# Batch 0 of a fused attention and maxout kernel: part of its up layer as block products, one PSUM copy in another place, its scores in 64x64 tiles

## The chip, the cores and the metric

The kernel runs on one core of a Trainium2 chip, as one launch. The metric is the device time of one execution in microseconds. The kernel before takes 320.29 us, the median of three runs (320.01 to 320.5).

## The reference

For each of 8 batches, 8 heads, 1024 positions and 64 features per head, keys and values are projected from 1024 positions to 64, attention runs over the 64 projected ones, and the heads are joined to rows x of 512 features. A layer of two products, their maximum and a third product follow.

```python
k_proj = np.einsum('ks,bhsd->bhkd', E, k)
v_proj = np.einsum('ks,bhsd->bhkd', F, v)
scores = scale * np.matmul(q, k_proj.transpose(0, 1, 3, 2))
...
attn = np.exp(scores)
attn = attn / (np.sum(attn, axis=-1, keepdims=True) + 1e-09)
x = np.matmul(attn, v_proj)
...
h1 = x @ w1
h2 = x @ w2
g = np.maximum(h1, h2)
out = g @ w_out
```

x has 8192 rows of 512 features, w1 and w2 are 512x1024, w_out is 1024x512, all inputs and the output float32. The kernel computes in float16 with float32 sums.

## The kernel before

**The algebra.** max(h1, h2) is written as relu(h1 − h2) + h2. So the kernel makes wd = w1 − w2 (`step_wd`, `step_wd_rows`), the *up layer* relu(x·wd), and M = w2·w_out once (`m_steps`); the *down layer* is relu(x·wd)·w_out + x·M, with x and the relu'd block joined along the contraction. For M, w2 is turned by TensorE transposes into a PSUM bank, and copied from there into `w2t_sb` by ScalarE (`step_w2t`, 256 of the 1024 columns at a time).

**Seven block products.** M, the down layer, and the up layer of batches 1 to 7 are computed by a scheme of the Strassen kind: both factors are cut into 2x2 blocks, seven products of sums of blocks replace the eight plain ones. They are called p1 to p7 and issued in the order 1, 2, 6, 5, 7, 3, 4. Three PSUM accumulators X, Y and Z hold them: X takes products 1, 6, 7 and 4 on top of each other and is copied to SBUF after each of the first three (`keep`, by ScalarE, into float32 tiles `p_sb`), Y takes product 2, Z products 5 and 3. VectorE adds the copies and the banks to the four result blocks. VectorE also prepares the sums: those of the weights once (`step_t` for w_out and M, `step_tw` for wd), those of x and of the relu'd block for every half batch (`sums_x`, `sums_g`), those of the turned w2 once (`sums_m`). In `up_steps` such a layer is done in two parts, d = 0 and d = 1: part d makes the columns of blocks 2d, 2d+1 (of 128) of either half of the 1024.

**Batch 0** is different: its up layer runs in the plain form (`up_slots`), eight blocks `u0[0]` to `u0[7]` for its first half of positions and `u1[0]` to `u1[7]` for the second, each of 4 matmuls of 128x128 against 512 columns into one bank, followed by a relu on ScalarE (on VectorE for block 3). The down layers of its two halves are `down_steps` of the units U[0, 0] and U[0, 1].

**PSUM.** Four banks are taken by `mm_bank`, by turns or by number, two double banks by turns by `att_banks`. A bank is written again only when its reader has finished.

**Order.** The order in which each engine issues is the program's order: the kernel is scheduled by hand. The list `slots` holds the steps of the steady part one after another; `at_slot` hangs further steps (sums, batch 1's attention, loads) behind a slot. The first 26 us (attention of batch 0) are written out line by line, with matmuls on ones (`warm`) between them. The list begins after that, with the rest of batch 0's up layer, the transposes of w2, and M; then the down layer of U[0, 0] follows in slots named ("P", 0, ...), with batch 1's attention hung behind them.

**Scores.** `score` computes exp's argument for four heads and 256 positions: for each head, both halves of the position tiles (`o`), a weight tile of the projected keys of 64 rows is cut into two of 32 columns, and each of these 16 tiles is a matmul of 64x32 against 256 columns. The 16 outputs lie in two banks. `step_sc` runs it for batches 0 and 1, `step_group` for the later ones.

**Transfers.** POOL's queue issues the loads: k, q, v of batch 0, the weights w2 and w1 in pieces, w_out, then batch 1's k, v, q and batch 2's k. SP's queue issues the check of the sums, the transposes of q by DMA in later batches, and the stores.

**Scratch.** `big0` to `big3` are SBUF tiles of 16 KB per partition. `big1` and `big2` first hold w1 and w2; after M's inputs are made, `open_box` takes them again under the same names for the sums (`s_g`, `s_x`), `big0` for the sums of wd (`t_w`), and `big3` holds `w2t_sb` and later sums of x.

## Time and profile before

| | |
|---|---|
| median of the runs | 320.29 us (320.01 to 320.5) |
| the profiled execution | 320.29 us, of which its span takes 318.5 us |
| TensorE (PE) busy | 311.8 us of the span |
| VectorE (DVE) busy | 241.1 us |
| ScalarE (ACT) busy | 206.0 us |
| granted TensorE clock | full speed in all 40 slices of the span |
| moved by DMA | 53.71 MB, 169 GB/s on average |

The profile is that of one execution. Its span runs from the first to the last record on the core; the time of the execution is 1.8 us more. A row of the chain of waits names the work that the end depended on, in order of time; a row of a timeline names an engine's instructions in order, with the idle time before them and what ended it in square brackets. "x16" is a count; "busy" includes the tail of a pipelined matmul, so that the rows of the chain, which do not overlap, are the ones to add up.

### The profile page before, as it was taken

The numbers are of one execution on the slowest core, as the hardware profiler recorded it, in microseconds if no ns is written. First come the engines' busy times: TensorE is split into PE (matmuls) and PEld (weight loads), VectorE is DVE, ScalarE is ACT, GpSimd is POOL, SyncE is SP. The second block draws the span as 40 slices with busy tenths as digits, with TensorE's granted clock in tenths as the row PEclk, the third lists the DMA queues.
The fourth block names the chain that finished last, engine by engine and source line by source line (L and its number), as shares of the span: only waits on it lengthen the run. The fifth ranks groups of instructions, "written<-read, shape, count | busy, mean of one in ns | idle before, by whom it ended". The sixth has DMA issues, their size and how long they took to land.

```text
span 318.5 us, 9309 instructions
## 1 busy us (share of the span) xinstructions
PE 311.8 (98%) x3922; PEld 253.8 (80%) x3922; DVE 241.1 (76%) x442; ACT 206.0 (65%) x373; POOL 41.4 (13%) x63
## 2 busy tenths in 40 slices
PE   7999999999999999999999999999999999999996
PEld 3565588888887888788887888788887888888885
DVE  2366889887969696896969696996969696969883
ACT  2386742777776777477776777477776777765541
POOL 8259102004000300012000400030000000000000
PEclk9999999999999999999999999999999999999999
DMA  7999999999989999799999999989979131313124
GB/s 179 206 202 197 207 207 201 207 156 141 204 163 183 171 209 245 208 188 147 225 229 219 169 199 245 221 155 174 230 153 217 42 101 36 102 35 102 36 99 136
DMA packets 76684, 53.71 MB, mean 169 GB/s; under 512 B 29664, under 2 KB 76128, under 8 KB 76640
## 3 DMA queue, kind: packets, MB, share of 16 engines
q0 software_dynamic: 30688, 28.05, 56.0%
q1 hardware_dynamic: 45664, 24.85, 33.1%
q8 instruction: 31, 0.51, 0.6%
q10 hardware_dynamic: 288, 0.20, 0.2%
q14 instruction: 13, 0.11, 0.1%
HBM read 57.15 MB, written 16.78 MB: 232 GB/s over the span
## 4 chain that ended last, share of the span: by engine, by line
PE 95%; DMA 3%; ACT 1%; DVE 1%; issue 0%; POOLq 0%
PE mm_ps L838 47%; PE mm_ps L746 27%; PE mm_ps L525 4%; PE mm_ps L195 4%; PE att_ps L352 4%; PE mm_ps L340 2%; DMA k_sb<-in_k_dram 2%; PE mm_ps L634 2%; PE att_ps L237 1%; PE mm_ps L311 1%; PE mm_ps L153 1%; DMA out_dram<-o_sb 1%; PE att_ps L340 0%; DVE qt_sb L316 0%; ACT ld_sb L388 0%
## 5 line engine op out<-in xcount | busy, mean ns | idle before, releaser
L720 ACT COPY p_sb<-mm_ps 128x512 f32<-128x512 f32 x179 | 101.7, 592 | 49.2 <-PE mm_ps L746 27.3
L838 PEld LDWEIGHTS <-big 128*128 128x128 f16 x768 | 73.5, 98 | 11.8 <-issue 3.6
L838 PE MATMUL mm_ps<-T_sb,big 128*128 128x256 f16 x576 | 76.9, 273 | 0.0
L761 DVE TENSOR_TENSOR gt_sb<-mm_ps,p_sb 128x512 f16<-128x512 f32 x56 | 38.5, 688 | 43.0 <-PE mm_ps L746 41.6
L746 PE MATMUL mm_ps<-big,big 128*128 128x256 f16 x336 | 50.4, 273 | 0.0
L746 PEld LDWEIGHTS <-big 128*128 128x128 f16 x448 | 43.8, 98 | 5.1
L838 PE MATMUL mm_ps<-wo_sb,gt_sb 128*128 128x256 f16 x256 | 42.6, 273 | 0.0
L838 PEld LDWEIGHTS <-gt_sb 128*128 128x128 f16 x376 | 35.7, 98 | 6.7 <-issue 2.7
L469 ACT ACTIVATE ex_sb<-mm_ps 128x512 f16<-128x512 f32 x50 | 27.2, 597 | 18.0 <-PE mm_ps L340 12.3
L746 PEld LDWEIGHTS <-wd_sb 128*128 128x128 f16 x336 | 32.9, 98 | 3.8
L746 PE MATMUL mm_ps<-xt_sb,wd_sb 128*128 128x256 f16 x224 | 32.8, 273 | 0.0
L499 DVE TENSOR_TENSOR xt_sb<-att_ps,ld_sb 128x1024 f16<-128x1024 f32 x26 | 31.7, 1219 | 0.2
L303 POOL COPY junk<-qt_sb 1x1 f16<-1x1 f16 x6 | 2.6, 432 | 172.3 <-DMA qt_sb<-q_sb 172.3
L838 PE MATMUL mm_ps<-m_sb,xt_sb 128*128 128x256 f16 x128 | 24.4, 273 | 0.0
L869 DVE TENSOR_TENSOR o_sb<-mm_ps,p_sb 128x512 f32<-128x512 f32 x32 | 21.9, 683 | 2.8 <-ACT p_sb L898 2.0
L764 DVE TENSOR_SCALAR gt_sb<-gt_sb 128x512 f16<-128x512 f16 (+1 forms) x60 | 20.9, 348 | 2.1
L706 DVE TENSOR_TENSOR big<-gt_sb 128x1024 f16<-128x1024 f16 x32 | 21.9, 683 | 0.0
L838 PE MATMUL mm_ps<-wo_sb,big 128*128 128x256 f16 x128 | 21.5, 273 | 0.0
L807 ACT ACTIVATE gt_sb<-mm_ps 128x512 f16<-128x512 f32 x28 | 16.8, 601 | 5.7 <-PE mm_ps L746 5.7
L838 PE MATMUL mm_ps<-T_sb,gt_sb 128*128 128x256 f16 x120 | 20.3, 273 | 0.0
L838 PEld LDWEIGHTS <-xt_sb 128*128 128x128 f16 x188 | 18.3, 98 | 2.3 <-issue 0.2
L761 DVE TENSOR_TENSOR gt_sb<-p_sb 128x512 f16<-128x512 f32 x28 | 19.1, 682 | 0.6 <-ACT p_sb L720 0.6
(121 smaller groups left out, 434.8 us busy)
## 6 DMA issues: line engine op xcount, KB each, us to landing
out_dram<-o_sb SPq DMA_DIRECT2D x62, 256.0 KB
k_sb<-in_k_dram POOLq DMA_DIRECT2D x7, 1024.0 KB, 9.7
v_sb<-in_v_dram POOLq DMA_DIRECT2D x7, 1024.0 KB, 15.4
q_sb<-in_q_dram POOLq DMA_DIRECT2D x5, 1024.0 KB, 22.8
q_sb<-in_q_dram POOLq DMA_DIRECT2D x6, 512.0 KB, 15.9
big<-in_moe_w_dram POOLq DMA_DIRECT2D x12, 128.0 KB, 6.4
v_sb<-in_v_dram POOLq DMA_DIRECT2D x4, 256.0 KB, 14.0
wo_sb<-in_moe_w_out_dram POOLq DMA_DIRECT2D x1, 1024.0 KB, 10.4
```

Source lines behind the costliest of these rows:

```text
L195: nc.tensor.matmul(out=kv_ps[r * KP : (r + 1) * KP, h * D : (h + nh) * D], lhsT=eft[i][:, c, :], rhs=t[w][:, h0 + h : h0 + h + nh, c, :], ...
L352: nc.tensor.matmul(out=dst(r ^ (hh % 2))[hh * Z : (hh + 1) * Z, :], lhsT=weights(rows, hh), rhs=ex[rows, hh % 2, hh // 2 * W : (hh // 2 + ...
L469: nc.scalar.activation(out=t["ex", g, j][:, e, :], in_=banks[e], func=ACTF.Exp, scale=scale)
L499: nc.vector.tensor_tensor(out=x_out(t, g, j).rearrange("q z o n -> q o z n"), in0=at_ps.rearrange("q o (z n) -> q o z n", z=2), in1=ld[:, ...
L706: nc.vector.tensor_tensor(out=S(i), in0=S(0) if x is None else x, in1=y(), op=op)
L720: copy(out=x, in_=bank)
L746: nc.tensor.matmul(out=bank[:, m * W : (m + 1) * W], lhsT=w_[:, n_, (2 * d + m) * 128 : (2 * d + m + 1) * 128], rhs=a[:, n_, :], start=(n ...
L761: nc.vector.tensor_tensor(out=c_blk(j, c), in0=two(x), in1=two(y), op=ALU.add)
L764: nc.vector.tensor_scalar_max(ap, ap, 0.0)
L807: nc.scalar.activation(out=out, in_=in_, func=ACTF.Relu)
L838: nc.tensor.matmul(out=bank[i][:, 0:CH] if two_banks else bank[:, i * CH : (i + 1) * CH], lhsT=a(c)[:, i * 128 : (i + 1) * 128], rhs=w_(c) ...
L869: nc.vector.tensor_tensor(out=o_sb, in0=two(x), in1=two(y), op=ALU.add)
```

## The change

Four things change, all in the part for batch 0 and M.

1. **Scores.** For batch 0 alone, `score` uses tiles of 64 columns, so that a call has 8 matmuls of 64x64 against 256 columns instead of 16 of 64x32. The other batches keep 32.
2. **Up layer.** Blocks 2, 3, 6 and 7 of `u1` are gone. They are computed by the seven products S1 to S7 of part d = 1 of `up_steps` for the unit U[0, 1]. Their copies go to tiles of the pool `soft` instead of `ppool`. S2's add and relu are held back (`c0`) and run as a slot of their own; the adds that follow S3 are held back too (`rest`) and run behind a slot of the down layer. The other blocks of batch 0 now take the banks 0 and 1 by turns (`fb % 2`), the products the banks 2 and 3.
3. **Order.** w2's second half (columns 512 to 1023) is turned earlier, right after S2, into the double banks; the second of its two copies by ScalarE is held back (`hold`) and issued behind the relu of `u0[4]`. Sums of x for U[0, 1], the differences of wd for d = 1 (`step_tw` now takes one part at a time), the sums for M and the differences of w_out stand in the list itself; sums for U[0, 0] move behind M's first products, and the differences of wd for d = 0 to the slots where U[0, 1]'s sums of x were. M's product 1 takes a double bank instead of bank 2, its product 2 bank 0, and its first add comes after product 6 (`M_add`).
4. **Scratch.** `s_g` and `s_x` lie in fixed columns of w1 and w2 instead of reopened tiles, since w1 and w2 are still partly read when the first sums are written.

```diff
@@ -335,11 +335,12 @@ score
-                    for s in range(2):
-                        pos = D * (o ^ e) + s * Z
+                    z = D if t is tiles[0] else Z
+                    for s in range(0, D, z):
+                        pos = D * (o ^ e) + s
                         nc.tensor.matmul(
-                            out=banks[e][pos : pos + Z, h * W : (h + 1) * W],
-                            lhsT=kpt_of(t, head, o)[:, s * Z : (s + 1) * Z],
+                            out=banks[e][pos : pos + z, h * W : (h + 1) * W],
+                            lhsT=kpt_of(t, head, o)[:, s : s + z],
...
@@ -518,7 +519,7 @@ up_slots
-                    t["up", j, fb] = mm_bank(n=None if r1 == NDC else first_banks[j][fb])
+                    t["up", j, fb] = mm_bank(n=first_banks[j][fb] if r1 < NDC else fb % 2)
...
@@ -560,9 +561,16 @@ step_w2t(f0, att=False, hold=False)
-        nc.scalar.copy(
-            out=w2t_sb[:, fb : fb + 2, :].rearrange("q f m -> q (f m)"), in_=ps_t
-        )
+
+        def copy():
+            nc.scalar.copy(
+                out=w2t_sb[:, fb : fb + 2, :].rearrange("q f m -> q (f m)"), in_=ps_t
+            )
+
+        if hold:
+            box["w2t"] = copy
+        else:
+            copy()
...
@@ -619,7 +627,7 @@ m_steps
-                st[name] = mm_bank(n=n)
+                st[name] = att_banks()[:, 0, :] if n == 3 else mm_bank(n=n)
...
-            st["s1"] = keep("pu", product(1, "X", 2))
+            st["s1"] = keep("pu", product(1, "X", 3))
...
-            add(0, 0, product(2, "Y", 3), st["s1"])
+            st["c0"] = product(2, "Y", 0)
...
-        return [p1, p2, p6, p5, p7, p3, p4]
+        return [p1, p2, p6, p5, p7, p3, p4, lambda: add(0, 0, st["c0"], st["s1"])]
 
     def s_g(i):
-        return box[2].rearrange("q (s n m) -> q s n m", s=4, n=NG)[:, i]
+        return (w1_sb, w2_sb)[i // 2][:, :, HALF + i % 2 * CH : HALF + (i % 2 + 1) * CH]
 
     def s_x(i, u):
         n = u["n"] % 3
-        half = box[1 if n < 2 else 3].rearrange("q (h s n m) -> q h s n m", h=2, s=4, n=NX)
-        return half[:, n % 2, i]
+        if n == 2:
+            return box[3].rearrange("q (h s n m) -> q h s n m", h=2, s=4, n=NX)[:, 0, i]
+        r = i % 2 * NX
+        return (w1_sb, w2_sb)[n][:, r : r + NX, i // 2 * CH : (i // 2 + 1) * CH]
...
-    def step_tw(i):
+    def step_tw(i, d):
+        f0 = d * CH
         sub4(
-            [t_w(i) for i in range(4)],
-            lambda h, c: wd_sb[:, h * NX : (h + 1) * NX, c * HALF : (c + 1) * HALF], (i,),
+            [t_w(i)[:, :, f0 : f0 + CH] for i in range(4)],
+            lambda h, c: wd_sb[:, h * NX : (h + 1) * NX, c * HALF + f0 : c * HALF + f0 + CH], (i,),
         )
...
@@ -716,18 +727,25 @@ keep, up_steps
-        x = ppool.tile([128, 512], FP32, tag=tag, bufs={"pu": 3, "pd": 4}[tag], name="p_sb")
+        if tag == "soft":
+            x = soft.tile([128, 512], FP32, tag=tag, name="p_sb")
+        else:
+            x = ppool.tile([128, 512], FP32, tag=tag, bufs={"pu": 3, "pd": 4}[tag], name="p_sb")
...
+    def up_gt(u):
+        return u["t"]["gt", u["o"]] if u["b"] == 0 else u["gt"]
...
-    def up_steps(u):
-        for d in range(2):
+    def up_steps(u, halves=range(2)):
+        for d in halves:
             st = {}
-            xbank, ybank = (2, 3) if d == 0 else (3, 2)
+            tag = "soft" if u["b"] == 0 else "pu"
+            xbank, ybank = (2, 3) if d == 0 or u["b"] == 0 else (3, 2)
...
-                add(0, 0, product(2, "Y", ybank), st["s1"])
-                relu(c_blk(0, 0))
...
+                bank = product(2, "Y", ybank)
+
+                def c0():
+                    add(0, 0, bank, st["s1"])
+                    relu(c_blk(0, 0))
+
+                if u["b"] == 0:
+                    u["c0"] = c0
+                else:
+                    c0()
...
                 bank = product(3, "Z", None)
+                if u["b"] == 0:
+                    def rest(u=u, st=st, d=d, bank=bank):
+                        add(0, 1, bank, st["u1"])
+                        add(1, 1, st["u2"], st["s5"])
+                        relu(up_gt(u)[:, NG + 2 * d : NG + 2 * d + 2, :])
+
+                    u["rest"] = rest
+                    return
...
@@ -1027,17 +1061,22 @@
+    open_box(0)
+    S1, S2, S6, S5, S7, S3, S4 = up_steps(U[0, 1], (1,))
+    M1, M2, M6, M5, M7, M3, M4, M_add = m_steps()
     slots = [
-        (0, lambda: u0[0](r0=2)), (1, lambda: u0[1](r0=2)), (None, lambda: loads(1, "v", "q", "k")),
-        (None, lambda: step_w2t(256, True)),
-        (2, lambda: u1[0](r0=2)), (3, lambda: u1[1](r0=2)),
-        (None, wd[1]), (4, u0[2]), (5, u0[3]),
-        (None, wd[2]), (6, u1[2]), (7, u1[3]), (None, wt[2]), (None, wt[3]), (8, u0[4]), (9, u0[5]), (None, wd[3]),
-        (10, u1[4]), (11, u1[5]), (12, u0[6]), (13, u0[7]),
-        (14, u1[6]), (15, u1[7]),
-        *((16 + n, x) for n, x in enumerate(m_steps())),
+        lambda: u0[0](r0=2), lambda: u0[1](r0=2), lambda: loads(1, "v", "q", "k"),
+        lambda: step_w2t(256, True),
+        lambda: u1[0](r0=2), lambda: u1[1](r0=2), wd[1], lambda: sums_x(U[0, 1], range(4)),
+        u0[2], u0[3], S1, S2, lambda: step_w2t(512, True), lambda: step_w2t(768, True, True), wd[2],
+        lambda: U[0, 1]["c0"](), u0[4], lambda: box.pop("w2t")(), u0[5], wd[3], lambda: [step_tw(i, 1) for i in range(4)] and None,
+        u1[4], S6, u1[5], S5, u0[6], S7, u0[7],
+        lambda: [sums_m(i) for i in range(4)] and None, S3, S4,
+        lambda: step_t(0, (0, 1)), M1, lambda: step_t(0, (2, 3)), M2, lambda: sums_x(U[0, 0], (0, 1)),
+        M6, lambda: sums_g(U[0, 0], (0, 1)), M_add, M5, lambda: sums_g(U[0, 0], (2, 3)), M7, M3, M4,
+        lambda: (open_box(3), new_attn(tiles[1]), turn.__setitem__(slice(None), [2, 3])) and None,
     ]
...
@@ -1069,23 +1108,12 @@
-        *((10 + i // 2, sums_m, i) for i in range(4)), *((12 + i, step_t, 0, (i,)) for i in range(4)),
-        (11, open_box, 1), (11, sums_x, U[0, 0], (0, 1)),
-        (15, open_box, 0, 2), (17, sums_x, U[0, 0], (2, 3)),
-        (18, sums_g, U[0, 0], (0, 1)), (19, sums_g, U[0, 0], (2, 3)), (22, open_box, 3),
...
@@ -1101,11 +1129,12 @@
-        if n in (2, 3):
-            for i in range(2):
-                at_slot(key, step_tw, 2 * (n - 2) + i)
+        if n == 2:
+            at_slot(key, sums_x, U[0, 0], (2, 3))
+        if n == 3:
+            at_slot(key, lambda: U[0, 1]["rest"]())
         if 6 <= n < 10:
-            at_slot(key, sums_x, U[0, 1], ((2, 0, 1, 3)[n - 6],))
+            at_slot(key, step_tw, n - 6, 0)
```

More of the change, by code (lines that the diff above doesn't have):

```diff
@@ L551, in step_wd_rows, with step_w2t @@
             )
-    def step_w2t(f0, att=False):
+    def step_w2t(f0, att=False, hold=False):
         ps_t = att_banks(FP16)[:, 0, :] if att else mm_bank(FP16)
@@ L757, in c_blk @@
             def c_blk(j, c, d=d):
[L758 removed]
+                return up_gt(u)[:, c * NG + 2 * d : c * NG + 2 * d + 2, j * W : (j + 1) * W]
             def add(j, c, x, y, c_blk=c_blk):
@@ L764, in relu, with p1, p6, p5 @@
                 nc.vector.tensor_scalar_max(ap, ap, 0.0)
-            def p1(st=st, product=product, xbank=xbank, d=d):
+            def p1(st=st, tag=tag, product=product, xbank=xbank, d=d):
                 if d == 0:
                     new_gt(u)
-                st["s1"] = keep("pu", product(1, "X", xbank))
+                st["s1"] = keep(tag, product(1, "X", xbank))
             def p2(st=st, product=product, ybank=ybank, add=add, c_blk=c_blk):
-                add(0, 0, product(2, "Y", ybank), st["s1"])
-                relu(c_blk(0, 0))
-            def p6(st=st, product=product):
-                st["u1"] = keep("pu", product(6, "X", None))
-            def p5(st=st, product=product, ybank=ybank):
-                st["s5"] = keep("pu", product(5, "Z", ybank))
-            def p7(st=st, product=product):
-                st["u2"] = keep("pu", product(7, "X", None))
+                bank = product(2, "Y", ybank)
[6 more added lines that the diff above has]
+                    c0()
+            def p6(st=st, tag=tag, product=product):
+                st["u1"] = keep(tag, product(6, "X", None))
+            def p5(st=st, tag=tag, product=product, ybank=ybank):
+                st["s5"] = keep(tag, product(5, "Z", ybank))
+            def p7(st=st, tag=tag, product=product):
+                st["u2"] = keep(tag, product(7, "X", None))
             def p3(st=st, product=product, add=add, c_blk=c_blk, d=d):
                 bank = product(3, "Z", None)
+                if u["b"] == 0:
[5 more added lines that the diff above has]
+                    return
                 if u["n"] == last:
@@ L1087 @@
     )):
-        key = ("P", n // 15, (n - 1) // 2 % 7, (n - 1) % 2) if n else (0, 22)
+        key = ("P", n // 15, (n - 1) // 2 % 7, (n - 1) % 2)
         for name in x.split():
```

8 lines of the change are left out of this document (1 added, 7 removed).

## The prediction

> **What bounds the kernel now.** I read the page first (busy time, chain of waits), then the table by stretches, then the chain in order of time where the diff changes something, and last each engine's timeline there.
>
> ```profile
> span 318.5 us, 9309 instructions
> ...
> PE 311.8 (98%) x3922; PEld 253.8 (80%) x3922; DVE 241.1 (76%) x442; ACT 206.0 (65%) x373; POOL 41.4 (13%) x63
> ...
> PE 95%; DMA 3%; ACT 1%; DVE 1%; issue 0%; POOLq 0%
> ```
>
> ```profile
> 0.00:23.90 23.90, 20.11 (x331) 12.03 (x332) 9.24 (x21) 11.05 (x16) 13.40 (x24) 1.00 1.12 195
> 23.90:314.00 290.10, 290.10 (x3574) 240.52 (x3575) 230.53 (x418) 194.77 (x357) 27.99 (x40) 1.00 0.89 166
> 314.00:318.50 4.50, 1.59 (x20) 1.26 (x18) 1.33 (x4) 0.20 (x1) 0.00 (x0) 1.00 0.57 182
> ```
>
> The columns are length, then busy time of PE, weight loads, DVE, ACT and POOL, clock, DMA share, GB/s. From 23.9 to 314.0 TensorE has no gap (290.10 of 290.10), at full clock. So in that stretch matmul time taken away or a wait put in reaches the end one to one, and removing waits of other engines is worth nothing. Only the first 23.9 us hold gaps (3.8 us).
>
> The chain in order of time (start, length, what; not adjacent to each other):
>
> ```profile
> 13.45 0.41 PE att_ps L340 x16
> ...
> 16.16 0.24 PE mm_ps L285 x8
> ...
> 18.50 0.34 PE att_ps L340 x16
> ...
> 27.48 4.32 PE mm_ps L525 x20
> 31.79 0.89 PE mm_ps L557 x16
> 32.69 6.91 PE mm_ps L525 x32
> 39.59 6.11 PE mm_ps L634 x56
> 45.70 3.27 PE mm_ps L838 x30
> ...
> 60.97 0.22 PE att_ps L340 x16
> ...
> 64.69 0.44 PE mm_ps L746 x4
> ```
>
> L525 is batch 0's up layer, L557 the transposes of w2, L634 the product M = w2·w_out, L838 the down layer, L746 an up layer by seven block products (later batches), L340 the scores. All of 27.48 to 45.70 is TensorE work end to end.
>
> **The up layer: the term that moves the time.** Blocks 2, 3, 6 and 7 of the second half of batch 0 go from 16 matmuls of 512 columns to 7 products of 4 matmuls of 256. L525 takes 6.91/32 = 0.216 us each: 16 are 3.46 us. L746 takes 0.437 us for 4 (0.109 each, weight loads included, since there as here each matmul has its own): 28 are 3.06 us. Removed 3.46, added 3.06: **0.40 us less**. The transposes and M keep their number.
>
> That arrives if no new wait appears. The changed program's order is known from its build, so I walk it with measured durations.
>
> ```profile
> 28.97 1.62 ACT L534 ACTIVATE gt_sb<-mm_ps 128x512 f16<-128x512 f32 x3
> ...
> 32.27 1.93 ACT L563 COPY big<-mm_ps 128x1024 f16<-128x1024 f16 x2 [0.71 <-PE mm_ps L557]
> ...
> 40.50 0.58 ACT L720 COPY p_sb<-mm_ps 128x512 f32<-128x512 f32 x1 [0.28 <-PE mm_ps L634]
> ```
>
> ```profile
> 30.10 0.69 DVE L536 TENSOR_SCALAR gt_sb<-mm_ps 128x512 f16<-128x512 f32 x1 [2.46 <-PE mm_ps L525]
> 30.71 0.84 DVE L549 TENSOR_TENSOR wd_sb<-big,big 128x512 f16<-128x512 f16 x2
> ...
> 34.23 0.69 DVE L706 TENSOR_TENSOR p_sb<-big 128x1024 f16<-128x1024 f16 x1 [1.05 <-ACT big L563]
> ...
> 36.78 0.42 DVE L706 TENSOR_TENSOR big<-xt_sb 128x512 f16<-128x512 f16 x1
> ...
> 66.11 0.69 DVE L761 TENSOR_TENSOR gt_sb<-mm_ps,p_sb 128x512 f16<-128x512 f32 x1 [0.29 <-PE mm_ps L746]
> 66.83 0.29 DVE L764 TENSOR_SCALAR gt_sb<-gt_sb 128x512 f16<-128x512 f16 x1
> ```
>
> TensorE, with 0.864 us per up block, 0.437 per product and 0.445 per eight transposes: the first half's blocks 2 and 3 end at 30.07 as before; S1 30.50, S2 30.93, the two transposes 31.38 and 31.83, block 4 32.69, block 5 33.56, the second half's block 4 34.42, S6 34.86, its block 5 35.72, S5 36.16, block 6 37.02, S7 37.46, block 7 38.32, S3 38.76, S4 39.20, against 39.59 before.
>
> *ScalarE* (0.54 per relu, 0.58 per copy of a product, 0.96 per copy of turned w2): relu of block 2 ends 30.59, S1's copy 31.17, first w2 copy 32.4, relu of block 4 33.3, second w2 copy 34.3, relu of block 5 34.85, then u1's block 4 35.4, S6 35.9. Two blocks share banks 0 and 1 by turns, so u1's block 4 (33.56) needs the relu that ends 33.3, and u1's block 5 (34.86) the one that ends 34.85: **margin nil**, the thinnest place. After it ScalarE gains 0.15 us per pair (1.15 of work against 1.30 of TensorE), so a slip does not grow. Behind that relu in ScalarE's queue stand S6's and S5's copies, which S7 (37.02) and S3 (38.32) need: 1 us of cover. I take 0 to 0.1 us of wait and put 0.02 in the sum. Here the held copy matters: unheld, w2's second copy would run 32.4 to 33.4, block 4's relu end at 33.95, and TensorE stand 0.4 us at 33.56. "Behind a relu" thus removes a wait the new order would have made, not one that is there now; its own worth against before is nothing.
>
> *VectorE*: the four sums of x (0.42 each) fall into the 2.46 us in which it waited before 30.10. Then block 3's relu to 30.79, w1−w2 for blocks 4 and 5 to 31.55 (needed 31.83, margin 0.28), S2's add and relu (0.69 + 0.29) to 32.5, where before another relu of 0.69 stood and ended at the same time, w1−w2 for blocks 6, 7 to 33.2, four differences of weights to 34.85 (S6 needs the second, at 34.05, by 34.42), the four sums of M (2.55 from 34.23 to 36.78 before) to 37.4, four differences of w_out (0.62 apart) to 39.9, two sums of x to 40.8, two of relu'd blocks (0.69 each) to 42.15. Only then comes the first add of M, which stood ahead of the latter before: it ends at 42.85. The copy of M's fifth product reuses the buffer that it reads and is due at 43.57; its bank is next used by the down layer at 45.3. Cover 0.7 us. The rest of the second half's adds (0.69 twice and 0.43) take the place of four weight differences of 0.69 around 48 us, and these come back as 0.42 each where the four sums stood. VectorE's busy share in these stages stays within some tenths of a us of before.
>
> **The transfers.** The transposes of w2's upper half stand 0.86 us earlier than 31.79.
>
> ```profile
> 22.68 1.42 POOL L139 DMA_DIRECT2D big<-in_moe_w_dram  x2
> ...
> big<-in_moe_w_dram POOLq DMA_DIRECT2D x2, 256.0 KB, 6.0
> ```
>
> Issued at 22.68 and 23.39 they land 6.0 us later, by 29.4; needed at 30.93: hidden. No issue changes its place in the POOL or SP queue, and none waits for anything new. The new scratch lies in w1 and w2 columns that are read out by then.
>
> ```profile
> 28.91 0.87 POOL L108 DMA_DIRECT2D v_sb<-in_v_dram  x1
> ...
> v_sb<-in_v_dram POOLq DMA_DIRECT2D x1, 1024.0 KB, 18.7
> ...
> 49.81 1.04 PE L237 MATMUL att_ps<-v_sb,eft 128*64 128x256 f16 x16
> ```
>
> Batch 1's v lands at 47.6 and is now wanted at 49.4 instead of 49.81: still hidden.
>
> **The scores.** Each of batch 0's four blocks goes from 16 matmuls of 64x32 to 8 of 64x64, 256 columns both. A block between others of its own shape takes 0.22 us (60.97), that is 16·0.109/8: eight run side by side. Alone among full-size matmuls it holds TensorE 0.34 (18.50), so entering the shape costs about 0.12. Four 64x64 tiles fill the array as eight 64x32 do, so two waves of 0.109 again: 0.22 + 0.12. The trace has no 64x64 tile with 256 columns; the nearest, L285 (64x64, 64 columns), does 8 in 0.24. Bounds: the entry cost vanishes (−0.12 for each of the two blocks on the chain), or tiles go two at a time (4·0.109 + 0.12 = 0.56, +0.22 each), or one at a time (+0.65 each). L285 does not decide between them: its tiles all lie in one half of the rows, and its 0.24 is four pairs of 0.027 plus an entry of 0.12, or eight single ones without. I take 0, nearest to the 64x32 rows, where both halves of rows and of columns do run together.
>
> The fourth block has 64x32 neighbours and now pays entry twice, 0.24 us. Its cover:
>
> ```profile
> 12.88 0.41 PE L340 MATMUL att_ps<-qt_sb,kpt_sb 64*32 64x256 f16 x16
> ...
> 13.45 0.41 PE L340 MATMUL att_ps<-qt_sb,kpt_sb 64*32 64x256 f16 x16 [0.16 <-DVE qt_sb L316]
> ...
> 19.98 0.30 PE L352 MATMUL att_ps<-ex_sb,ones 64*32 64x256 f16 x8
> 20.09 0.41 PE L340 MATMUL att_ps<-qt_sb,kpt_sb 64*32 64x256 f16 x16
> ...
> 21.92 0.30 PE L352 MATMUL att_ps<-ex_sb,ones 64*32 64x256 f16 x8 [0.28 <-ACT ex_sb L380]
> ```
>
> TensorE waits 0.28 us for ScalarE behind the fourth block: just hidden; without that cover, +0.24. The Trainium skill, "TensorEngine Tiling (Array Packing)", Key Properties, says that changing the tiling mode drains TensorE; the 0.34 against 0.22 agrees, and by that rule too the fourth block pays twice and the others as now.
>
> **The sum.** 318.5 − 0.40 + 0.02 = 318.1 us of span. The profiled execution took 320.29, 1.8 us around its span, and is itself the median of the three runs (320.01 to 320.5). So 319.9 us.
>
> **The rivals.**
> 1. *Slower: the 64x64 tiles do not run side by side*, at 12.9 to 20.5 us. For: two row halves write the same bank. Against: the 64x32 form does that too, in 0.22. One at a time: +0.65 three times, less 0.16 of idle at the first, +0.6 at the fourth, −0.4: 322.3. It turns slower than before from 0.2 us per block on. Two at a time: +0.44 − 0.40, no change, 320.3. The Trainium skill, same page, Gotcha 1, says different row tiles cannot access one bank at a time, which would give the two-at-a-time case; the 0.22 row speaks against it.
> 2. *The saving goes into waits* at 31.8 and 34.86, or for the late add of M: ScalarE or VectorE 0.2 to 0.4 us later than my walk. For: nil margin. Against: earlier relus are timed here. 320.1 to 320.3; with both and M's add late, 320.9.
> 3. *Hidden anyway*: a load sets the pace later on. For: DMA share 0.89. Against: no gap after 23.9. 320.3.
> 4. *Better: the entry cost shrinks too*, half the weight loads: −0.24 more, 319.65 or a little less.
>
> **How the numbers follow.** Forecast 0.58; rival 1: 0.06 one at a time, 0.05 two at a time; rival 2: 0.16; rival 3: 0.04; rival 4: 0.11. Time 319.9. Range 319.3 to 320.9: it takes in rivals 2, 3 and 4, with the runs' spread below, and the paired case. About 0.2% (0.64 us) is what a measurement here tells from no change: faster needs under 319.65, which is two thirds of rival 4 and a quarter of the forecast, by the runs' spread of 0.25: 0.22; slower needs over 320.93: the single-file case, a third of rival 2, and 0.05 of the forecast for a wait that my walk overlooks: 0.16; the rest, 0.62, is no change.
>
> **What would show it.** Right: PE busy falls to about 311.4; M starts at 39.2; score blocks of 8 hold TensorE 0.34; no PE wait over 0.1 us after 23.9. Wrong: a score block over 0.5 us; PE idle before the second half's block 5 naming ScalarE, or before block 4 naming wd_sb; an M copy that waits for VectorE; the first gap-free stretch beginning later than 23.9.

## The result and the profile after

The changed kernel takes 320.97 us (median of 16 runs, 320.43 to 324.49) beside 319.97 us for the kernel before (16 runs): a ratio of 1.0043, 95% interval 1.0027 to 1.0059. It is 1.0 us slower; the forecast was no change at 319.9, and the time lies just outside the range that ended at 320.9. A few runs of most kernels here, with 64x64 tiles and with 64x32 alike, show a granted clock of 0.995 or less and take some 1 to 5 us more than the rest, so medians are compared, and for the run both_pe below, where six of twelve executions are of that kind, the median of the other six, 320.27 us, is used too.

The profiled execution took 321.01 us. First the page's head, of the changed kernel:

```profile
span 319.2 us, 9285 instructions
...
PE 312.1 (98%) x3902; PEld 254.8 (80%) x3902; DVE 244.6 (77%) x450; ACT 206.9 (65%) x375; POOL 39.6 (12%) x63
```

Busy totals tell little here. The table by stretches does, cut where the first up block starts, where the down layer starts, and ahead of the last stage. Before the change (columns as in the prediction):

```profile
0.00:23.82 23.82, 20.03 (x331) 11.95 (x331) 9.16 (x21) 11.05 (x16) 13.32 (x24) 1.00 1.11 195
23.82:45.70 21.88, 21.88 (x162) 13.69 (x155) 16.44 (x32) 13.82 (x22) 8.35 (x11) 1.00 1.29 204
45.70:313.90 268.20, 268.20 (x3422) 226.82 (x3420) 214.16 (x388) 180.84 (x335) 19.72 (x29) 1.00 0.85 163
313.90:318.50 4.60, 1.69 (x21) 1.35 (x19) 1.34 (x5) 0.30 (x1) 0.00 (x0) 1.00 0.56 178
```

and after it:

```profile
0.00:23.66 23.66, 20.50 (x298) 11.91 (x299) 9.15 (x20) 11.05 (x16) 13.07 (x24) 1.00 1.13 195
23.66:45.69 22.03, 21.67 (x174) 14.73 (x167) 19.71 (x40) 14.70 (x24) 8.60 (x11) 1.00 1.28 201
45.69:313.90 268.21, 268.21 (x3421) 226.73 (x3420) 214.44 (x388) 180.81 (x335) 17.95 (x29) 1.00 0.87 163
313.90:319.20 5.30, 1.74 (x22) 1.40 (x19) 1.30 (x5) 0.34 (x1) 0.00 (x0) 1.00 0.49 155
```

The four stretches differ by −0.16, +0.15, +0.01 and +0.70 us. The 268 us in which TensorE's work was not changed are the same. The stretch that was to be 0.4 us shorter is 0.15 longer, and TensorE is idle in it for 0.36 us (21.67 of 22.03). The largest loss is where nothing was changed at all: the last 5 us.

**The stretch with the up layer.** The chain in order of time, after (start, length, what):

```profile
24.85 6.28 DMA big<-in_moe_w_dram
...
31.23 0.06 DVE wd_sb L550
...
31.57 0.69 DVE gt_sb L779
...
32.91 0.75 DVE wd_sb L550 x2
...
34.15 0.44 DVE big L605
...
34.63 0.61 PE mm_ps L764 x4
```

L764 at 34.63 is S6. It ends a chain that runs back over VectorE (the second weight difference L605, w1−w2 L550, S2's add L779) to the transfer of w1 that landed at 31.13. Before, all of this stretch was TensorE. The timeline of all engines there, after:

```profile
31.23 0.43 DVE L550 TENSOR_TENSOR wd_sb<-big,big 128x512 f16<-128x512 f16 x1 [0.26 <-DMA big<-in_moe_w_dram]
...
31.98 0.89 POOL L108 DMA_DIRECT2D k_sb<-in_k_dram  x1
32.29 0.70 DVE L782 TENSOR_SCALAR gt_sb<-gt_sb 128x512 f16<-128x512 f16 x1
...
34.63 0.61 PE L764 MATMUL mm_ps<-big,big 128*128 128x256 f16 x4 [0.36 <-DVE big L605]
```

Two things are later than the walk in the prediction: w1−w2 waits 0.26 us for w1, and S2's relu (L782) takes 0.70 us where the row it was priced by says 0.29. It runs while POOL issues batch 2's k (31.98 to 32.87).

**The last stage.** The last three adds of VectorE and the last matmul, before and after:

```profile
314.85 0.91 DVE L937 TENSOR_TENSOR o_sb<-mm_ps,p_sb 128x256 f32<-128x256 f32 x3 [0.29 <-PE mm_ps L931]
...
316.62 0.16 PE L1196 MATMUL mm_ps<-ones 128*1 128x1 f16 x1 [1.19 <-DMA out_dram<-o_sb]
```

```profile
315.26 0.82 DVE L971 TENSOR_TENSOR o_sb<-mm_ps,p_sb 128x256 f32<-128x256 f32 x3 [0.66 <-PE mm_ps L965]
...
316.93 0.16 PE L1225 MATMUL mm_ps<-ones 128*1 128x1 f16 x1 [1.45 <-DMA out_dram<-o_sb]
```

VectorE's first add starts 0.41 us later, though the matmuls it waits for stand only 0.04 later; its idle time grows from 0.29 to 0.66. What it waits for by the program was done by 314.8 (TensorE's product, started at 314.42 and 0.38 long; ScalarE's copy earlier). From the last matmul to the span's end there are 1.90 us before and 2.24 after. Counted from the program's start, with waits for semaphores and the like, this add is VectorE's instruction number 564 before and number 576 after, because the change puts 12 more ahead of it.

The scores are as forecast. After:

```profile
17.82 0.41 PE L341 MATMUL att_ps<-qt_sb,kpt_sb 64*64 64x256 f16 x8
18.16 0.64 PE L195 MATMUL mm_ps<-v_sb,eft 128*64 128x128 f16 x16
...
20.02 0.41 PE L341 MATMUL att_ps<-qt_sb,kpt_sb 64*64 64x256 f16 x8
20.36 0.63 PE L353 MATMUL mm_ps<-ex_sb,vp_sb 64*32 64x256 f16 x32
...
21.73 0.30 PE L353 MATMUL att_ps<-ex_sb,ones 64*32 64x256 f16 x8 [0.16 <-ACT ex_sb L381]
```

A block of eight 64x64 matmuls holds TensorE 0.34 us (17.82 to 18.16, 20.02 to 20.36), and the fourth block's second entry is taken out of the wait for ScalarE, 0.16 where it was 0.28.

### The profile page after: what moved, and what is told of

Same layout as the page of the kernel before. It is cut to its first block, busy times and chain, and to the rows that moved or that the text cites. A ratio compares the mean times of both kernels' runs of the same rounds, so it can differ in the third digit from the quotient of the medians.

```text
span 319.2 us, 9285 instructions
## 1 busy us (share of the span) xinstructions
PE 312.1 (98%) x3902; PEld 254.8 (80%) x3902; DVE 244.6 (77%) x450; ACT 206.9 (65%) x375; POOL 39.6 (12%) x63
## 4 chain that ended last, share of the span: by engine, by line
PE 88%; DMA 7%; POOL 3%; DVE 1%; issue 1%; POOLq 0%; DVEq 0%
PE mm_ps L872 47%; PE mm_ps L764 28%; DMA v_sb<-in_v_dram 5%; PE att_ps L353 3%; PE mm_ps L195 3%; PE mm_ps L341 3%; DMA big<-in_moe_w_dram 2%; PE att_ps L237 1%; PE att_ps L642 1%; POOL big L139 1%; PE mm_ps L642 1%; PE mm_ps L526 1%; DMA out_dram<-o_sb 1%; POOL v_sb L108 1%; PE mm_ps L311 1%
## 5 line engine op out<-in xcount | busy, mean ns | idle before, releaser
L872 PEld LDWEIGHTS <-big 128*128 128x128 f16 x768 | 73.5, 98 | 11.8 <-issue 3.6
L779 DVE TENSOR_TENSOR gt_sb<-mm_ps,p_sb 128x512 f16<-128x512 f32 x58 | 39.8, 687 | 42.1 <-PE mm_ps L764 40.7
L764 PE MATMUL mm_ps<-big,big 128*128 128x256 f16 x348 | 52.2, 273 | 0.4 <-DVE big L605 0.4
L764 PEld LDWEIGHTS <-big 128*128 128x128 f16 x464 | 45.3, 98 | 6.5 <-DVE big L605 0.9
L764 PEld LDWEIGHTS <-wd_sb 128*128 128x128 f16 x348 | 34.0, 98 | 4.4
L764 PE MATMUL mm_ps<-xt_sb,wd_sb 128*128 128x256 f16 x232 | 33.8, 273 | 0.0
L782 DVE TENSOR_SCALAR gt_sb<-gt_sb 128x512 f16<-128x512 f16 (+1 forms) x62 | 23.0, 371 | 2.1
L303 POOL COPY junk<-qt_sb 1x1 f16<-1x1 f16 x6 | 1.1, 191 | 169.5 <-DMA qt_sb<-q_sb 169.5
L779 DVE TENSOR_TENSOR gt_sb<-p_sb 128x512 f16<-128x512 f32 x29 | 19.8, 681 | 0.6 <-ACT p_sb L734 0.6
```

What stands on the lines that cost most here:

```text
L764: nc.tensor.matmul(out=bank[:, m * W : (m + 1) * W], lhsT=w_[:, n_, (2 * d + m) * 128 : (2 * d + m + 1) * 128], rhs=a[:, n_, :], start=(n ...
L779: nc.vector.tensor_tensor(out=c_blk(j, c), in0=two(x), in1=two(y), op=ALU.add)
L782: nc.vector.tensor_scalar_max(ap, ap, 0.0)
L872: nc.tensor.matmul(out=bank[i][:, 0:CH] if two_banks else bank[:, i * CH : (i + 1) * CH], lhsT=a(c)[:, i * 128 : (i + 1) * 128], rhs=w_(c) ...
```

## The experiments

All are compared with the kernel before run beside them. "Up stretch" is from the first up block to M's first matmul in the profile, 15.61 us before (23.82 to 39.43). Line numbers shift by a few where lines are added.

| run | median us | kernel before beside it | ratio, 95% | up stretch us |
|---|---|---|---|---|
| again | 321.34 | 320.15 | 1.0046 (1.0019 to 1.0072) | 15.91 |
| pad_before | 320.81 | 320.15 | 1.0015 (0.9998 to 1.0031) | 15.61 |
| pad_after | 320.28 | 320.15 | 1.0010 (0.9984 to 1.0036) | 15.48 |
| c0_late | 321.12 | 320.15 | 1.0033 (1.0010 to 1.0057) | 15.30 |
| tt_relu | 319.91 | 319.85 | 0.9995 (0.9975 to 1.0015) | 15.30 |
| both | 319.93 | 319.85 | 1.0001 (0.9969 to 1.0032) | 15.30 |
| sc32 | 320.40 | 319.85 | 1.0010 (0.9991 to 1.0029) | 15.80 |
| sc64_before | 320.69 | 319.85 | 1.0013 (0.9993 to 1.0032) | 15.61 |
| both_again | 319.73 | 319.96 | 0.9986 (0.9969 to 1.0003) | 15.30 |
| both32 | 320.50 | 319.96 | 1.0014 (0.9991 to 1.0037) | 15.30 |
| unheld | 320.22 | 319.96 | 0.9995 (0.9973 to 1.0018) | 15.72 |
| sc64_pad | 320.75 | 319.96 | 1.0011 (0.9987 to 1.0035) | 15.61 |
| both_pe | 321.26 | 320.32 | 1.0044 (1.0016 to 1.0073) | 15.30 |
| both32_pe | 320.99 | 320.32 | 1.0041 (1.0024 to 1.0059) | 15.29 |
| sc64_pe | 320.16 | 320.32 | 1.0001 (0.9986 to 1.0017) | 15.61 |
| sc64_look | 320.97 | 320.32 | 1.0025 (1.0004 to 1.0045) | 15.61 |

### again: the changed kernel once more

> The changed kernel once more, as the measure for the runs beside it. Both theories: about 1.0 us over the kernel before (1.003 to 1.004). Lateness theory (VectorE is late ahead of the second half's S6, and its first add of the last stage starts late): TensorE waits 0.3 to 0.4 us ahead of S6 at 34.6 us, M starts at 39.6 and not at 39.2, and VectorE's first add of the last stage (line 971) starts about 0.4 us after its TensorE work is done. Rival (the profiled run was a disturbed one): neither of the two waits comes back, M starts at 39.2, and the time lies within 0.3 us of the kernel before.

Both waits came back: VectorE's last adds with 0.66 us of idle time, S6 with 0.52, and the up stretch at 15.91. The lateness is the kernel's, not one execution's.

### The last stage: pad_before and pad_after

```diff
     wd_sb = const.tile([128, NDC, DF], FP16)
+    for _ in range(8):
+        nc.vector.memset(wd_sb[:, 0, 0:8], 0.0)
```

(twelve in pad_before).

> The kernel before with twelve small memsets on VectorE at 2.9 us, which put the first add of its last stage at number 576 of VectorE's program, as in the changed kernel. Theory (place in the program): idle time ahead of that add grows from 0.29 to about 0.66 us, the span's end comes 0.4 to 0.6 us later, time 320.4 to 320.6 with the rest of the trace unchanged. Rival (something the change does to data or queues): the add starts as in the kernel before, and the time stays at 320.0 (1.000).

> Eight small memsets on VectorE at 2.9 us, where it is idle, move every later VectorE instruction eight places on. The first add of the last stage is then number 584 of VectorE's program and not 576; number 576 is then one with 2 us of idle time ahead of it. Theory (the add started 0.4 us late because of its place in VectorE's program: its instruction was fetched late, at a place that is a multiple of 64): the add starts right behind its TensorE work, the span's end comes 0.4 to 0.6 us earlier, the time falls by 0.4 to 0.6 against the changed kernel, to about 320.4. Rival (the add waits for a store or for ScalarE): 0.66 us of idle time ahead of it stays, the time stays within 0.1 us of the changed kernel's. The wait ahead of S6 is untouched under both.

The last adds of pad_before (L939), then of pad_after (L973), with the last matmul:

```profile
315.54 0.82 DVE L939 TENSOR_TENSOR o_sb<-mm_ps,p_sb 128x256 f32<-128x256 f32 x3 [0.66 <-PE mm_ps L933]
...
317.23 0.16 PE L1198 MATMUL mm_ps<-ones 128*1 128x1 f16 x1 [1.48 <-DMA out_dram<-o_sb]
```

```profile
314.57 0.90 DVE L973 TENSOR_TENSOR o_sb<-mm_ps,p_sb 128x256 f32<-128x256 f32 x3 [0.29 <-PE mm_ps L967]
...
316.33 0.16 PE L1227 MATMUL mm_ps<-ones 128*1 128x1 f16 x1 [1.19 <-DMA out_dram<-o_sb]
```

Twelve dummy instructions in the kernel before, 310 us ahead of the end, give it the same 0.66 us and cost 0.66 us in the median; eight in the changed kernel take the 0.66 away, and its median falls by 1.06 against the unchanged one beside it. So the place of the add in VectorE's program makes it late, not its data. In the traces, M's first matmul to the span's end takes 279.09 us before and in pad_after, and 279.75 to 279.87 in the four kernels with the add at number 576. So the last stage is worth 0.66 to 0.78 us; the rest of the 1.06 goes with the wait ahead of S6, which was shorter in pad_after (up stretch 15.48 against 15.91).

One more view belongs to it, the DMA queues of the changed kernel from 315 to 317 us:

```profile
q1 hardware_dynamic: 399, 0.37, 55.9%
q10 hardware_dynamic: 162, 0.14, 21.9%
q14 instruction: 1, 0.01, 1.7%
```

The third row is a packet of the queue that brings instructions. In pad_after no such row stands between 315 and 317; one stands between 309 and 311 instead, where VectorE has 2 us to wait anyway. In the changed kernel the packet lies between 316.2 and 316.6 us:

```profile
q14 instruction: 1, 0.01, 8.6%
```

It starts at 316.31, 1.05 us behind the start of the late add (315.26), and in again, pad_before and c0_late it starts 1.03 to 1.06 us behind it. So VectorE did not wait for this packet. The place in the program and a fetch go together; what holds the add back for 0.37 us stays open. The Trainium skill, "Runtime: NRT & Kernel Launch", Instruction fetch mechanics, says that fetching runs in blocks alongside execution and that crossing a block is mostly hidden. If number 576 is such a crossing, the 0.37 us (0.66 less 0.29) are a case in which it was not hidden.

### The wait ahead of S6: c0_late and tt_relu

```diff
-        lambda: U[0, 1]["c0"](), u0[4], lambda: box.pop("w2t")(), u0[5], wd[3], lambda: [step_tw(i, 1) for i in range(4)] and None,
+        u0[4], lambda: box.pop("w2t")(), u0[5], wd[3], lambda: [step_tw(i, 1) for i in range(4)] and None,
+        lambda: U[0, 1]["c0"](),
```

> S2's add and relu on VectorE stand behind the four weight differences instead of ahead of wd[3]. If S6 waits because these two stand ahead of the weight differences (0.69 + 0.70 us measured), the differences end about 1 us earlier, S6 starts without a wait, and M starts 0.3 to 0.4 us earlier, at 39.2 to 39.3; the time falls by as much against the changed kernel (about 320.6). New wait possible: S5 writes the bank that the late add reads, at 35.7, and the add would end by 34.5 to 35.0: none. Rival (TensorE waits for w1's or w2's transfer and not for VectorE's order): the wait ahead of S6 stays at 0.3 us and M starts at 39.6. The tail is as in the changed kernel under both.

In c0_late the up stretch is 15.30 us, S6 starts without a wait, and S2's relu at its later place takes 0.29 us again. The last adds keep their 0.66 us of idle time, as they should: they are still number 576. The median fell by only 0.22 us against the changed kernel run beside it, where 0.3 to 0.4 was expected; runs that spread over 2 us can't tell the two apart, and the 0.6 us of the profiles (15.91 to 15.30) is the clearer reading.

tt_relu has the eight memsets and one more for the zeros, and leaves S2's relu where it is but writes it with two tensors:

```diff
-                    relu(c_blk(0, 0))
+                        nc.vector.tensor_tensor(out=c, in0=c, in1=z, op=ALU.max)
```

> The eight memsets, and S2's relu alone as a maximum of two tensors (the second one zeros) and not with a constant; its place is that of the changed kernel. Theory (that relu takes 0.70 us and not 0.29 because in its form VectorE can't run while POOL writes the descriptors of batch 2's k, issued at 31.98 for 0.89 us): the two-tensor form takes 0.42 to 0.50 us at the same place, the weight differences end about 0.2 to 0.3 us earlier, and S6 starts as much earlier. Rival 1 (any VectorE instruction is slow there): it takes 0.7 us or more. Rival 2 (the relu waits for something): it starts or ends where it did, about 32.65. In time 0.2 us or less against the kernel with memsets alone, 320.0 to 320.3.

The timeline of tt_relu:

```profile
31.68 0.90 POOL L108 DMA_DIRECT2D k_sb<-in_k_dram  x1
...
31.97 0.43 DVE L801 TENSOR_TENSOR gt_sb<-gt_sb,ident 128x512 f16<-128x512 f16 x1
...
34.04 0.61 PE L768 MATMUL mm_ps<-big,big 128*128 128x256 f16 x4
```

POOL writes the same descriptors at the same time, the relu takes 0.43 us, the row of S6 names no wait, and the up stretch is 15.30. So it is the form of the relu under POOL's work that is slow, not VectorE as a whole, and not a wait for data. The Trainium skill, "SBUF — State Buffer", Who interferes with whom, says that a tensor_scalar can enter a mode that needs the port pair VectorE shares with GpSimd, held exclusively for a whole instruction, and that a tensor_tensor has no such mode. The 0.70 against 0.43 and 0.29 agree.

What the relu alone is worth shows beside pad_after, which has the slow form and in which VectorE hardly waits for w1:

```profile
32.01 0.71 DVE L784 TENSOR_SCALAR gt_sb<-gt_sb 128x512 f16<-128x512 f16 x1
...
34.36 0.61 PE L766 MATMUL mm_ps<-big,big 128*128 128x256 f16 x4
```

S6 starts 10.70 us after the first up block there, 10.52 us in tt_relu, and 10.44 us in c0_late. So the relu is worth 0.18 us of the up stretch (15.48 against 15.30). The rest of the loss goes with w1. The piece that w1−w2 waits for landed 7.20 us after the first up block in pad_after, 7.47 in the changed kernel and 7.63 in again; S6 started 3.49 to 3.50 us behind it each time, and the up stretch was 15.48, 15.75 and 15.91. In tt_relu the piece landed at 7.30, so this run does not show that another form of the relu alone mends the loss when w1 lands late. In c0_late, both and both_again it landed at 7.43 to 7.51 and S6 still started at 10.44: with the add and the relu behind the differences, a late landing costs nothing.

### Both mended: both, both_again

> S2's add and relu behind the weight differences, and the eight memsets at 2.9 us. If both losses are told rightly they are independent: no wait ahead of S6 (the stretch from the first up block to M takes 15.2 to 15.3 us, against 15.61 before and 15.75 in the changed kernel), no late add in the last stage (0.29 us of idle time ahead of it), and the time is 0.3 to 0.5 us under the kernel before: 319.6 to 319.9, the forecast of the prediction. Rival (the gain goes into a further wait down the line, or the first 23.9 us take longer with the changed scores): 320.0 or more, with the stretch to M at 15.2 us all the same.

> The kernel with S2's add and relu late and eight memsets once more, as the measure for its neighbour with 64x32 tiles. Both theories: 319.8 to 320.0, M starts 15.3 us after the first up block.

TensorE's timeline in both_again:

```profile
33.82 0.60 PE L766 MATMUL mm_ps<-big,big 128*128 128x256 f16 x4
34.34 1.02 PE L528 MATMUL mm_ps<-xt_sb,wd_sb 128*128 128x512 f16 x4
...
38.68 1.04 PE L644 MATMUL att_ps<-wo_sb,big 128*128 128x256 f16 x8
```

S6 starts at 33.82 and its 4·0.109 us end at 34.26; the second half's block 5 starts at 34.34. That 0.08 is all that is left between the walk and the run. From the first up block to the span's end it takes 294.39 us in both_again and in both, against 294.70 before. In time the two stand +0.08 and −0.23 us to the kernel before, each interval holding 1.000: the saving of 0.3 us is seen in the traces and can't be told from no change in the times. No version here beats the kernel before beyond doubt.

### The held copy: unheld

both, with the second copy of turned w2 issued at once.

```diff
-        lambda: step_w2t(768, True, True)
+        lambda: step_w2t(768, True)
...
-        u0[4], lambda: box.pop("w2t")(), u0[5]
+        u0[4], u0[5]
```

> S2's add and relu late, eight memsets, and the second copy of turned w2 not held back: it stands ahead of the relu of block 4 on ScalarE. By the prediction TensorE then waits 0.4 us where the second half's block 4 takes its bank (2.6 us after the first up block that follows the transposes less one block: at about 33.0 here), naming ScalarE; M starts 15.6 to 15.7 us after the first up block instead of 15.3, and the time is 0.3 to 0.4 us over the held one's. Rival (holding back was worth nothing, since VectorE's weight differences are as late as the relu): M at 15.3 to 15.4, the time the same.

```profile
33.62 1.02 PE L528 MATMUL mm_ps<-xt_sb,wd_sb 128*128 128x512 f16 x4 [0.34 <-ACT gt_sb L537]
```

The wait stands where the prediction put it and names ScalarE's relu; the up stretch grows from 15.30 to 15.72. In time it is 0.5 us over its neighbour both_again.

### The scores and the length of TensorE's program

sc32 is the changed kernel with the eight memsets and 64x32 tiles (`z = Z`), both32 the same on top of both; sc64_before is the kernel before with the scores' part of the change alone, sc64_pad the same with twenty memsets.

> The changed kernel with the eight memsets, and batch 0's scores back in 64x32 tiles (so without the first part of the change). By the prediction the tiles are worth 0: the time is that of the kernel with memsets alone (about 320.3) within 0.2 us, a block of 16 holds TensorE 0.34 us as a block of 8 does. Rival 1 (64x64 brings the first stage forward): the first up block starts 0.2 to 0.5 us later than with 64x64. Rival 2 (64x64 tiles make the clock fall in some runs, which the changed kernel shows more often than the kernel before): no run with a granted clock under 0.997, where 64x64 had it in about one of six.

> The kernel before with batch 0's scores in 64x64 tiles and nothing else of the change. By the prediction: 320.0 to 320.2, no change (ratio 1.000), a score block holding 0.34 us. Rival 1: the first up block starts 0.2 us or more earlier than 23.8 us after the span's start and the time falls as much. Rival 2 (clock): one run in six with a granted clock under 0.997 and 1.5 us or more over the others.

> S2's add and relu late, eight memsets, and batch 0's scores in 64x32 tiles: two of the three parts of the change, without its two losses. Theory A (64x64 tiles are worth nothing, the first 23.9 us differ by chance of the transfers): within 0.2 us of the same kernel with 64x64 tiles, which runs beside it; from the first up block to the span's end 294.4 us under both. Theory B (64x64 tiles cost time that the profile's look at a single execution missed: the kernel before took 320.69 with them against 319.85): 0.4 to 0.8 us faster than its neighbour, 319.2 to 319.5, and 0.1 to 0.2% faster than the kernel before.

> The kernel before with 64x64 score tiles and twenty memsets on VectorE, which put the first add of its last stage at number 584, where it is not late. Theory A (the 0.7 us that 64x64 tiles alone seemed to cost belong to how that build's first transfers land, before any score): the first up block starts 15.2 to 15.3 us after the first product on k, as before, and the time is 319.9 to 320.3. Theory B (64x64 tiles cost time): 320.5 to 320.9 again.

sc32 is 0.55 us over the kernel before, where pad_after with 64x64 tiles was 0.13 over its own. These runs speak against a price of the tile as such: with 64x64 tiles the kernel before stands 0.84 and 0.79 us over the unchanged one (each interval holds 1.000), and the mended kernel with 64x32 tiles, both32, stands 0.77 us over both_again. What they share is a program of TensorE that is 64 instructions longer or shorter (8 matmuls with their weight loads, four blocks). Three runs change that length and keep the tiles of a kernel above: the matmuls on ones of the first stage are cut into narrower ones.

```diff
-        for _ in range(n):
+        for i in range(n):
+            m = 171 if n == 8 and i < 6 else 256
+            for a in range(0, 512, m):
+                b = min(512, a + m)
...
-                out=w_ps, lhsT=ones16[:, 0:128], rhs=ones16, start=True, stop=True
+                    out=w_ps[:, a:b], lhsT=ones16[:, 0:128], rhs=ones16[:, a:b], start=True, stop=True
```

> The kernel before with 64x64 tiles and the matmuls on ones cut, so that TensorE's program is again as long as in the kernel before. Theory (place): the 0.8 us are gone, 319.8 to 320.1, ratio 1.000. Rival 1 (the tiles' shape costs it in the first stage): 320.6 to 320.8. Rival 2 (neither: the first transfers land later in some builds for a reason that no instruction shows): either, with the first product on k late where the time is.

> The kernel before with 64x64 tiles alone, once more. Theory (place): 320.6 to 320.8 again, and the profile shows the loss either in the first 24 us ahead of the first score (first product on k at 8.9 us, as in the first look) or by a fetch among the stores (first up block to the end over 294.7 us). Rival (chance of two runs): 319.9 to 320.1.

> S2's add and relu late, eight memsets, 64x64 tiles, and the first stage's matmuls on ones cut into narrower ones of the same columns in all, so that TensorE's program has 64 instructions more from there on, as with 64x32 tiles. Theory (place in TensorE's program): a fetch of 16 KB falls at 313.4 among the last stores, the last matmul waits 1.7 to 2.0 us for its store instead of 1.2, and the time is 0.5 to 0.8 us over that of the uncut kernel: 320.2 to 320.6. Rival (the tiles' shape): no fetch matters, 319.7 to 319.9.

> The same with 64x32 tiles: 128 instructions more than with 64x64 tiles uncut. TensorE fetches 256 instructions at a time and takes 14 us for them there, so 64 more move the fetch from 313.4 to about 309.9, ahead of the last stores. Theory (place): the last matmul waits 1.2 us, from the first up block to the end 294.4 us, time 319.7 to 319.9. Rival (the tiles' shape): 320.5 as with 64x32 tiles uncut.

For the kernel before it fits: with 64x64 tiles and the old length the time is 320.16 beside 320.32, with 64x64 tiles alone 320.97. So 64x64 tiles do not by themselves cost the 0.8 us there. The shorter program does, or the narrower matmuls on ones win as much; these runs do not part the two. Where the time goes is not settled. The up stretch and the end are as before (294.70 us from the first up block on, in sc64_before and in sc64_look), so it is lost in the first 24 us; but the profile of a typical run (sc64_before) shows the first product on k at 8.91 us behind a late transfer, ahead of every changed instruction. The profiled executions of sc64_pad (319.86 us) and sc64_look (320.26 us) lie 0.7 to 0.9 us under the medians of their runs and can't show the loss; in sc64_pad the first up block started 16.0 us after the first product on k, and not 15.2 to 15.3 as expected.

For the mended kernel it fits in part. With 64x32 tiles, TensorE's fetch falls among the last stores. The DMA queues of both32 from 312 to 317 us, and its last matmul:

```profile
q8 instruction: 1, 0.02, 1.7%
```

```profile
316.66 0.16 PE L1228 MATMUL mm_ps<-ones 128*1 128x1 f16 x1 [1.69 <-DMA out_dram<-o_sb]
```

both_again has no such packet in that window, and its last matmul waits 1.19 us. In both32_pe, 64 instructions longer still, the wait is 1.20 again and 294.38 us pass from the first up block to the end, as expected; but its median is 320.99. In its profile the first up block starts at 24.33 us, where both_again has 23.38, so something is lost earlier. One such loss is in TensorE's timeline:

```profile
23.00 0.50 PE L356 MATMUL att_ps<-ex_sb,vp_sb 64*32 64x256 f16 x19 [0.47 <-ACT vp_sb L210]
23.99 0.40 PE L356 MATMUL att_ps<-ex_sb,vp_sb 64*32 64x256 f16 x13 [0.48 <-issue]
```

In the middle of 32 short matmuls TensorE stands 0.48 us for nothing that the profile shows; no other run here has that. And both_pe, which should have been as late as both32, has the fetch among its stores and a wait of only 1.23 us, and the median of its other six runs, 320.27, is no later than the kernel before beside it (320.32). So in both_pe and both32_pe the expectation failed. That the length of TensorE's program decides half a microsecond either way is argued from sc64_pe and from the fetch in both32 and in sc32, whose last matmul waits 1.95 us; it is not shown.

## Why the prediction was wrong

**The up layer's 0.40 us: right.** With the two losses mended the up stretch is 15.30 against 15.61, 0.31 less: the 0.40 less 0.08 of wait ahead of the second half's block 5, where the prediction saw a margin of nil, allowed 0 to 0.1 and put 0.02.

**VectorE ahead of S6: the first step that failed.** The walk gave a margin of 0.37 us (second weight difference ready at 34.05, needed by 34.42). Counted from the first up block, the difference was ready at 10.23 us in the walk, at 10.64 in pad_after and at 10.91 in the changed kernel. The first 0.41 us are one mis-sized term: S2's relu, 0.29 in the walk and 0.70 in the run, because it was priced by a row at 66.83 us, where POOL issues nothing, and put at a place where POOL writes the descriptors of k. The row that would have told it stood in POOL's timeline of before,

```profile
31.90 0.89 POOL L108 DMA_DIRECT2D k_sb<-in_k_dram  x1
```

and the prediction read that queue for its transfers only.

The other 0.27 us are VectorE's wait for w1 (0.26 in the timeline of the changed kernel). The walk took the measured end of w1−w2 (31.55) and did not see that a transfer set it: the piece of w1 landed at 31.04 before, 7.22 us after the first up block, and at 31.13 in the changed kernel, 7.47 us after it. The 29.4 of the prediction is the landing of w2's upper half, which came at 29.73. How late w1 lands differs between executions (7.47 and 7.63 us in the same kernel), so this part of the loss is in part chance.

The margin was also smaller than 0.37. The walk counted TensorE by the chain, whose times run 0.16 us behind the starts in the timeline (M at 39.59 in the chain and 39.43 in the timeline, before), and VectorE by the timeline. Where nothing holds S6 it starts 10.44 us after the first up block (both_again), and not 10.60 as in the walk.

**Rival 2** (the saving goes into waits of VectorE or ScalarE, 320.1 to 320.3) had this mechanism at other places and about this price, with a chance of 0.16. It was the right story for the 0.4 us, told too small a chance, and not the story of the rest.

**The end: a term that the sum lacked.** The sum was made of durations and waits; that an edit 280 us earlier shifts every later instruction of its engine by twelve places was priced at nothing without a word. From M's first matmul to the span's end it cost 0.66 us in the changed kernel, 0.76 in again and 0.73 in pad_before, more than anything else. The late add makes 0.37 to 0.43 of it. Another 0.34 to 0.49 come behind the last matmul (2.24 to 2.39 us to the span's end, against 1.90), and what makes them is open. Without this term rival 2's 320.1 to 320.3 would have held in the number: pad_after took 320.28, beside 320.15 for the kernel before.

**The scores: right for the tile, wrong for the kernel around it.** 0.34 us per block and the hidden fourth entry came as forecast. But with 64x64 tiles the kernel before was 0.65 to 0.84 us slower and the mended kernel 0.77 us faster than with 64x32, which no rival had. That the 64 instructions fewer of TensorE's program make both is argued, not shown.

**The held copy: right.** "Behind a relu" removes a wait of 0.4 us that the new order would have made; unheld measured 0.42.

**What would show it.** M's first matmul stands 15.75 us after the first up block (23.66 to 39.41) where the forecast of 0.38 us less made 15.23; the wait after 23.9 us was there, and it named VectorE (wd_sb's differences), as the prediction's list of bad signs has it but for the place. PE busy was a bad sign: 312.1 and not 311.4, half a microsecond of it in the first stage (20.50 against 20.03), where idle time depends on when k and v land. No wait came from M's late add, batch 1's v or the early transposes: 45.7 to 313.9 took 268.21 us against 268.20.

## What to carry to other kernels

Price a VectorE instruction at the place where it will stand, with what POOL does at that time, and not by the same form elsewhere: a margin put at 0.37 us was lost to one relu that took 0.41 us more, and to a transfer that the walk did not see. And count instructions, not only their time: in a kernel tuned to tenths of a microsecond an edit moves every later instruction of its engine, and a handful of dummies at an idle place is the test that tells such a shift from a real cost, in either direction. When an experiment's two contexts give a part opposite signs, as the scores did here, it is not that part alone that is being measured.

## What was unexpected of the hardware

- VectorE's instruction number 576 starts 0.37 us late in the four traces where it is the first add of the last stage (the changed kernel, again, c0_late, pad_before), and no add there is late in the other fourteen, where the number is 564, 584 or 585. A packet of instructions follows about 1.05 us behind the late add, so it is not what the add waits for.
- A relu of 128x512 float16 from SBUF to SBUF takes 0.29 us, and 0.70 to 0.71 while POOL writes descriptors, ending 0.10 to 0.12 us behind POOL's instruction (the changed kernel, again, pad_after, sc32); as a maximum of two tensors at the same place it takes 0.43.
- TensorE stood 0.48 us between two short matmuls of one group with nothing to wait for (both32_pe at 23.5 us), after its program had been made longer by 128 instructions.
